# Banded attention with a gated layer: heads regrouped, w_in loaded over 128 partitions, batch 0 turned over in 64x64 blocks

## The chip, the cores and the metric

The kernel runs on one core of a Trainium2 chip. The metric is the device time in microseconds (us) from start to end of one execution. TensorE is the matrix engine, VectorE, ScalarE and GpSimd work on vectors, and SyncE (SP) issues all of the kernel's transfers; 16 DMA engines carry them.

## The reference

Eight batches, 8 heads, 576 positions, head dimension 64. Each query attends to at most 32 keys: its own position and those before it (heads 0 to 3: the last 32 positions; heads 4 to 7: every fourth position of the last 128). The heads' outputs side by side are the input x (576 x 512) of a gated layer.

```python
scores = np.where(masks, scale * q @ k.T, -1e9)
attn = softmax(scores)                      # per head, banded
x = (attn @ v), heads side by side          # B, 576, 512
h = np.maximum(x @ w_in, 0.0)               # 512 -> 1024
u, v = h[..., :512], h[..., 512:]
v_n = (v - mean(v)) / np.sqrt(var(v) + 1e-6)
v_s = w_spatial @ v_n + b_spatial           # mixes the 576 positions
out = (u * v_s) @ w_out                     # 512 -> 512
```

w_in and w_out reach the kernel as 8-byte numbers, so w_in is 4 MB and a half row of 512 numbers is 4096 bytes.

## The kernel before

**Order of the work.** Each piece of work is a Python generator, a strand: `heads_in` and `values_in` (loads), `unit` (scores and softmax), `weighted` (probabilities times values), `v_tile`, `gate` and `project` (the gated layer), `piece_in`, `weight`, `spatial_in`, `spatial`, `weight_in` (loading and splitting of the weights). Class `Timeline` keeps a clock for each engine, with an assumed cost for each step (the numbers behind `yield PE`, `yield ACT` and so on), gives out buffers (eight PSUM banks, four key buffers, six `mid` tiles) and emits the instructions in the order in which its clocks run them. Each strand has a rank; the table SHIFTS moves single ranks, LOADS orders the first loads, BY_POOL and EXTRA choose the engine for some steps (in BY_POOL 'a' and 's' put the addition and the subtraction of the splitting on GpSimd, and without the letter they run on VectorE). The engines work their instructions in that order. All transfers go through SP's one queue, in order as well; an issue waits for its buffer and holds up those behind it.

**Attention.** Heads lie in pairs; `heads_in` loads the keys and queries of a pair, transposed, two heads of 64 rows over 128 partitions, in two transfers (lines 560 and 561). Two pairs form a group; a batch has groups 0 and 1. `unit` computes the scores of a third of a group: 96 products of 64x32 (line 599), maximum, exponential, sum (L689), reciprocal, division (L693). The probabilities have the queries on partitions, 64 of each pair of the group, and along the row first the head j in the pair, then 64 keys. `turn` turns them over with three 128x128 transposes (L614) into one PSUM bank, and ScalarE copies it out (L706). `weighted` (L749) multiplies with the values: the product for head j of the two pairs i = 0, 1 goes to partitions 64 i, so chunk 2G + j of x holds one head of each of two pairs. The values of batch 0 are loaded by pair in four transfers of 32 partitions, both heads' columns to the partitions of each head j, so each byte comes twice (L575). Later batches load only the columns of the head that is used (L586).

**Weights.** As the chunks of x hold the heads in that order, the rows of w_in that belong to a chunk are two blocks of 64 rows that do not adjoin. `piece_in` loads each of the four chunks of each half in two transfers of 64 partitions, the very first block in five parts. `weight` then splits a piece into a high and a low part: two steps on ScalarE (L448, L478), two on VectorE (L452, L454), an addition (L461 on GpSimd or L464 on VectorE), a rounding (L483), a subtraction (L381 or L378). `spatial` splits w_spatial (L510, then L381 or L378). The staging buffers of w_spatial and w_out come free as pieces of w_in are read.

**Gated layer.** Each product is formed in three passes of high and low parts: `v_tile` (L814), `gate` (L881, L891 to L893), `project` (L916). `warm` (L938) fills TensorE at the start with dummy products.

Of the kernel before, what the change touches and what calls it, by code (L numbers as in the profile page):

```python
# [59 lines left out]
LOADS = [0, 1, 3, 20, 2, 10, 21, 4, 5, 15, 8, 6, 13, 9, 12, 18, 7, 22, 23, 11, 19, 17, 26, 24, 16, 14, 25]  # L60
BY_POOL = {
    (0, 0): 's', (0, 1): 'as', (0, 2): 's', (0, 3): 's', (1, 0): 'as', (1, 1): 's',
    (1, 2): 'as', (1, 3): 'a', (2, 0): 'a', (2, 1): 'a', (2, 2): 'as', (2, 3): 'as',
}
EXTRA = {
    ('soft', 0, 0, 0): 0, ('soft', 0, 0, 1): 0, ('soft', 0, 0, 2): 0, ('soft', 0, 1, 0): 0, ('soft', 0, 1, 1): 0, ('soft', 0, 1, 2): 0,
    ('soft', 1, 0, 0): 0, ('soft', 1, 0, 1): 0, ('soft', 1, 0, 2): 0, ('soft', 1, 1, 0): 0, ('soft', 1, 1, 1): 1, ('soft', 1, 1, 2): 1,
    ('sp', 0): 1, ('sp', 1): 1, ('sp', 2): 1, ('sp', 3): 1, ('sp', 4): 1, ('vn', 0): 0,
    ('vn', 1): 1, ('vn', 2): 0, ('vn', 3): 0, ('vn', 4): 1,
# [159 lines left out]
def tile_banded_attention_gated_moe(  # L229
# [157 lines left out]
    def piece_in(half, c):  # L387

        yield DMA, 1.5, 1.1 if half == 0 or c else 2.1
        dtype = w_in.dtype  # L390
        words = NF if dtype == F32 else 2 * NF
        tile = stage[c // 2 + 2 * (1 - half)]
        place = tile[:, c % 2 * BIG :][:, :words] if half else tile[:, c % 2 * words :][:, :words]
        for n in range(2):
            row = (c // 2 * 4 + c % 2 + 2 * n) * D
            cuts = (0, 8, 16, 24, 32, D) if half and c == 0 and n == 0 else (0, D)
            for lo, hi in zip(cuts, cuts[1:]):
                nc.sync.dma_start(  # L398
                    place[n * D + lo : n * D + hi].bitcast(dtype), w_in[row + lo : row + hi, half]
                )  # L400
        staged["wi", half, c] = place
        if half:
            slots["wi", half, c] = [("stage", tile[:, c % 2 * BIG : c % 2 * BIG + BIG])]
        tl.done("in", "wi", half, c)
# [142 lines left out]
    def heads_in(b, hp, lo=0, hi=NU):  # L547

        if lo == 0:
            yield "kq"  # L550
        else:
            yield [("qk", b, hp, lo - 1)]
        got = yield DMA, 0.52 * (hi - lo), 0.87
        if lo == 0:
            used[b, hp] = got
            keys[b, hp] = got[0][1]
        kq = keys[b, hp]
        w = S // NU
        kc = slice(lo * w + WIN * (lo > 0), hi * w + WIN)
        nc.sync.dma_start(kq[:, kc], kT[b, hp, :, kc])  # L560
        nc.sync.dma_start(
            kq[:, WIN + S + lo * w : WIN + S + hi * w].rearrange("p (u c) -> p u c", c=w), qT[b, hp, :, lo:hi]
        )
        for u in range(lo, hi):
            tl.done("qk", b, hp, u)

    def values_in(b, hp):

        if b == 0:
            yield DMA, 1.6, 1.6  # L570
            dst = wide[hp // 2][:, hp % 2 * BIG : hp % 2 * BIG + BIG]
            for j in range(2):
                for n in range(2):
                    k = WIN + (1 - n) * QB
                    nc.sync.dma_start(dst[j * D + n * QB : j * D + n * QB + QB], vw[b, hp, k : k + QB])  # L575
            values[b, hp] = [dst.rearrange("p (t j d) -> p t j d", j=2, d=D)[:, :, j] for j in range(2)]
            tl.done("values", b, hp)
            return
        yield "val"
        (big,) = yield DMA, 1.33, 3.0  # L580
        src = vw[b, hp].rearrange("k (t j d) -> k t j d", j=2, d=D)
        dst = big[1].rearrange("p (t d) -> p t d", d=D)
        for j in range(2):
            for n in range(2):
                k = WIN + (1 - n) * QB
                nc.sync.dma_start(dst[j * D + n * QB : j * D + n * QB + QB], src[k : k + QB, :, j, :])  # L586
        values[b, hp] = [dst, dst]
# [23 lines left out]
    def turn(pp, p, u):  # L611

        for e in range(US):
            nc.tensor.transpose(pp[:, e * P : e * P + P], p[:, e].rearrange("p j k -> p (j k)"), ident)  # L614

    def unit(b, G, u):
# [76 lines left out]
        nc.gpsimd.tensor_mul(flat, flat, rv.unsqueeze(2).broadcast_to([P, 2 * US, KW]))  # L693
        if u:
            yield [("turned", b, G)]
            yield "pt bank"
        else:
            yield "pt bank pT"
        held = yield PE, 0.53, 6
# [3 lines left out]
        turn(held[1][1], p, 0)  # L703
        tl.give(pb)
        yield ACT, 0.48
        nc.scalar.copy(probs[b, G][1][:, u * US * P : u * US * P + US * P], held[1][1][:, : US * P])  # L706
# [5 lines left out]
    def weighted(b, G, rank):  # L712
# [6 lines left out]
        for phase in range(2):  # L719
# [14 lines left out]
            for work_now in itertools.zip_longest(*runs):  # L734
                for odd, h, kb, blocks in filter(None, work_now):
                    row = (1 - odd) * QB
                    for j in (1, 0) if phase else (0, 1):
                        r = slice(j * D + row, j * D + row + QB)
                        for i, hp in enumerate(pairs):
# [5 lines left out]
                            else:  # L745
# [5 lines left out]
                                values[b, hp][j][r, kb // 2],  # L751
# [197 lines left out]
    first += [heads_in(0, 2), heads_in(0, 3), piece_in(1, 0), values_in(0, 0), values_in(0, 1), piece_in(1, 1)]  # L949
    first += [piece_in(1, 2), values_in(0, 2), values_in(0, 3), piece_in(1, 3)] + [piece_in(0, c) for c in range(NC)]  # L950
# [97 lines left out]
```

## Time and profile before

| | us |
|---|---|
| three runs: median (lowest to highest) | 567.3 (565.21 to 569.45) |
| the profiled execution | 566.32 |
| its span, first to last instruction | 564.5 |
| TensorE busy | 540.7 (96%) |
| VectorE busy | 291.1 (52%) |
| ScalarE busy | 222.5 (39%) |
| GpSimd busy | 134.4 (24%) |
| mean granted clock of TensorE, as a share | 0.984 |

Busy times are shares of one span and overlap between engines. Matmuls are pipelined, so a busy TensorE need not be at its peak; a granted clock of 1.00 is 2.4 GHz, 0.50 is 1.2 GHz. What counts is which engine or transfer the others wait for in a stretch, and the stretches differ, so the rows below go by stretch.

### The profile page before, as it was taken

To read this page: it belongs to the slowest core of one execution; us is meant where nothing else is said; L and a number is where in the kernel's file an instruction comes from. 1 tells how busy PE (TensorE), PEld (TensorE's weight loads), DVE (VectorE), ACT (ScalarE), POOL (GpSimd) and SP (SyncE) were. 2 spreads that over 40 slices of the span, in tenths; PEclk is the share of its full clock that TensorE was granted. 3 is DMA by queue.
4 is the path that set the end of the run, shared out by engine and by line. 5 is a ranking of instruction groups with operands and counts; after the bars stand their busy time and mean duration, and the time that the engine had idled before them with its cause. 6 is when DMAs were issued, how large, how long until landed. Compare 5 with 4: busy or idle time off the path is not lost.

```text
span 564.5 us, 18030 instructions
## 1 busy us (share of the span) xinstructions
PE 540.7 (96%) x7838; PEld 496.7 (88%) x7838; DVE 291.1 (52%) x732; ACT 222.5 (39%) x558; POOL 134.4 (24%) x164
## 2 busy tenths in 40 slices
PE   7668988999999999999999999999999999999997
PEld 5446878987999898998998999899999988999997
DVE  6547996547554576555235756566321437314220
ACT  3545765434333353234423344335221424224122
POOL 3446763312223223222001513232100003000000
PEclk9868999999999999999999999999999999999999
DMA  8898622333203424033211342310201100000102
GB/s 244 210 252 226 207 82 88 123 106 79 83 1 121 141 52 134 12 110 129 76 34 27 104 141 66 120 44 2 76 33 43 44 34 1 12 21 12 43 22 74
DMA packets 58818, 48.38 MB, mean 86 GB/s; under 512 B 39154, under 2 KB 48370, under 8 KB 58740
## 3 DMA queue, kind: packets, MB, share of 16 engines
q1 hardware_dynamic: 58740, 47.24, 29.0%
q8 instruction: 61, 1.00, 0.7%
q14 instruction: 17, 0.14, 0.1%
HBM read 37.79 MB, written 9.44 MB: 84 GB/s over the span
## 4 chain that ended last, share of the span: by engine, by line
PE 81%; DMA 10%; DVE 4%; SPq 3%; issue 1%; POOL 1%; ACT 0%; ACTq 0%
PE bank L916 18%; PE bank L891 17%; PE bank L881 17%; PE bank L814 15%; PE bank L749 5%; PE bank L599 4%; DMA kq<-in_qT_dram 3%; DMA wideh<-in_vw_dram 3%; PE bank L614 2%; PE bank L893 1%; PE bank L892 1%; DMA stage<-in_w_spT_dram 1%; DMA wosl<-in_w_in_dram 1%; DMA stage<-in_w_in_dram 1%; SPq L398 1%
## 5 line engine op out<-in xcount | busy, mean ns | idle before, releaser
L881 PE MATMUL bank<-xth,wih 128*128 128x288 f32 x256 | 77.3, 302 | 0.0
L916 PE MATMUL bank<-gh,woh 128*128 128x288 f32 x256 | 77.1, 301 | 0.0
L891 PE MATMUL bank<-wth,vnh 128*128 128x288 f32 x256 | 77.0, 301 | 0.1
L896 DVE TENSOR_TENSOR ur<-ur,bank 128x288 f32<-128x288 f32 x64 | 28.8, 451 | 93.2 <-PE bank L893 90.2
L891 PE MATMUL bank<-wth,vnl 128*128 128x288 f32 x256 | 75.4, 295 | 0.0
L916 PE MATMUL bank<-gl,woh 128*128 128x288 f32 x256 | 75.4, 295 | 0.0
L891 PE MATMUL bank<-wtl,vnh 128*128 128x288 f32 x256 | 75.4, 295 | 0.0
L881 PE MATMUL bank<-xtl,wih 128*128 128x288 f32 x256 | 75.4, 295 | 0.0
L916 PE MATMUL bank<-gh,wol 128*128 128x288 f32 x256 | 75.4, 295 | 0.0
L881 PE MATMUL bank<-xth,wil 128*128 128x288 f32 x256 | 75.4, 294 | 0.0
L832 POOL TENSOR_TENSOR stats<-stats,halfneg 128x1 f32<-128x1 f32 (+1 forms) x37 | 26.2, 709 | 156.8 <-DVE stats L830 156.3
L814 PE MATMUL bank<-wih,xth 128*128 128x512 f32 (+1 forms) x148 | 61.2, 414 | 0.0
L693 POOL TENSOR_TENSOR pg<-pg,rv 128x384 f32<-128x384 f32 x48 | 41.5, 865 | 77.2 <-DVE rv L691 62.7
L814 PE MATMUL bank<-wih,xtl 128*128 128x512 f32 (+1 forms) x148 | 58.6, 396 | 0.0
L814 PE MATMUL bank<-wil,xth 128*128 128x512 f32 (+1 forms) x148 | 58.5, 396 | 0.0
L684 POOL TENSOR_TENSOR pg<-pg,nm 128x384 f32<-128x384 f32 x36 | 30.9, 858 | 113.0 <-DVE nm L682 107.9
L884 ACT ACTIVATE ur<-bank 128x288 f32<-128x288 f32 x64 | 26.3, 412 | 65.3 <-PE bank L881 65.2
L902 ACT CAST gh<-ur 128x288 fp32r<-128x288 f32 x64 | 26.8, 433 | 62.2 <-DVE ur L896 53.2
L891 PEld LDWEIGHTS bank<-wth,vnh 128*128 128x128 f32 x256 | 48.1, 188 | 1.0 <-ACT ur L884 0.3
L916 PEld LDWEIGHTS bank<-gh,woh 128*128 128x128 f32 x256 | 48.1, 188 | 0.9
L881 PEld LDWEIGHTS bank<-xth,wih 128*128 128x128 f32 x256 | 48.1, 188 | 0.7
L920 ACT COPY ob<-bank 128x288 f32<-128x288 f32 x64 | 25.6, 401 | 57.8 <-PE bank L916 48.2
(116 smaller groups left out, 1116.4 us busy)
## 6 DMA issues: line engine op xcount, KB each, us to landing
kq<-in_kT_dram SPq DMA_DIRECT2D x30, 304.0 KB
kq<-in_qT_dram SPq DMA_DIRECT2D x30, 288.0 KB
val<-in_vw_dram SPq DMA_DIRECT2D x112, 72.0 KB
out_dram<-ob SPq DMA_DIRECT2D x48, 144.0 KB
stage<-in_w_out_dram SPq DMA_DIRECT2D x4, 512.0 KB
stage<-in_w_in_dram SPq DMA_DIRECT2D x7, 256.0 KB
out_dram<-ob SPq DMA_DIRECT2D x16, 112.0 KB
stage<-in_w_spT_dram SPq DMA_DIRECT2D x5, 288.0 KB
```

The costliest lines, as they stand in the source:

```text
L684: nc.gpsimd.tensor_add(flat, flat, nm.unsqueeze(2).broadcast_to([P, 2 * US, KW]))
L693: nc.gpsimd.tensor_mul(flat, flat, rv.unsqueeze(2).broadcast_to([P, 2 * US, KW]))
L749: nc.tensor.matmul(acc[h, j][1][1][i * D : i * D + D, at : at + len(blocks) * QB], values[b, hp][j][r, kb // 2], x, start=phase == 0 and k ...
L814: nc.tensor.matmul(pm, xt[a][:, c, at : at + m], wi[w][:, c, NF:], start=c == 0 and n == 0, stop=c == NC - 1 and n == 2)
L832: nc.gpsimd.tensor_tensor(rs[:m], rs[:m], halfneg[:m], op=ALU.pow)
L881: nc.tensor.matmul(pu, wi[w][:, c, fs], xt[a][:, c, xs], start=n == 0, stop=n == 3 * NC - 1)
L884: nc.scalar.activation(ur, pu, AF.Relu)
L891: nc.tensor.matmul(pv, vn[c][a][:, fs], wts[w][:, c, ws], start=n == 0, stop=False)
L896: nc.vector.tensor_mul(ur, ur, pv)
L902: nc.scalar.copy(gated[0][:, f, ts], ur)
L916: nc.tensor.matmul(po, wo[w][:, f, ds], gated[a][:, f, ts], start=n == 0, stop=n == 3 * NC - 1)
L920: nc.scalar.copy(ob[1], po)
```

## The change

Chunk c of x now holds heads 2c and 2c + 1, so a piece of w_in is 128 rows that adjoin, loaded in one transfer over 128 partitions. For this the kernel puts one head of each of two pairs together.
In batches 1 to 7 `heads_in` does it while loading: keys and queries come in four transfers of 64 partitions instead of two of 128, and the values' row blocks now go by pair. In batch 0 (`WHOLE = 1`) keys and queries are loaded as before, and `turn` does the regrouping: 12 products of 64x64 with the identity per unit, into two PSUM banks, each bank's half copied out by itself (two copies of 64 partitions). The values of batch 0 are loaded once per group (8 transfers instead of 16).
The tables are new: SHIFTS, LOADS, BY_POOL (additions on GpSimd: 6 instead of 8; subtractions: 9 as before) and EXTRA (unit ('soft', 1, 1, 1) goes by matrix product, ('sp', 2) to VectorE, ('vn', 0) and ('vn', 1) exchanged, one of the six new copies to VectorE).

```diff
-LOADS = [0, 1, 3, 20, 2, 10, 21, 4, 5, 15, 8, 6, 13, 9, 12, 18, 7, 22, 23, 11, 19, 17, 26, 24, 16, 14, 25]
+LOADS = [0, 1, 3, 2, 19, 5, 6, 4, 17, 18, 7, 9, 10, 20, 12, 16, 14, 15, 23, 8, 22, 11, 21, 13, 24]
 BY_POOL = {
-    (0, 0): 's', (0, 1): 'as', (0, 2): 's', (0, 3): 's', (1, 0): 'as', (1, 1): 's',
-    (1, 2): 'as', (1, 3): 'a', (2, 0): 'a', (2, 1): 'a', (2, 2): 'as', (2, 3): 'as',
+    (0, 0): 'as', (0, 1): 'as', (0, 2): 'as', (0, 3): '', (1, 0): 's', (1, 1): 's',
+    (1, 2): 'as', (1, 3): 's', (2, 0): '', (2, 1): 'as', (2, 2): 'a', (2, 3): 's',
 }
+WHOLE = 1
 ...
     def piece_in(half, c):
 ...
-        for n in range(2):
-            row = (c // 2 * 4 + c % 2 + 2 * n) * D
-            cuts = (0, 8, 16, 24, 32, D) if half and c == 0 and n == 0 else (0, D)
-            for lo, hi in zip(cuts, cuts[1:]):
-                nc.sync.dma_start(
-                    place[n * D + lo : n * D + hi].bitcast(dtype), w_in[row + lo : row + hi, half]
-                )
+        nc.sync.dma_start(place.bitcast(dtype), w_in[c * P : c * P + P, half])
 ...
     def heads_in(b, hp, lo=0, hi=NU):
 ...
+        whole = b < WHOLE
 ...
-        nc.sync.dma_start(kq[:, kc], kT[b, hp, :, kc])
-        nc.sync.dma_start(
-            kq[:, WIN + S + lo * w : WIN + S + hi * w].rearrange("p (u c) -> p u c", c=w), qT[b, hp, :, lo:hi]
-        )
+        rows = slice(hp % 2 * D, hp % 2 * D + D)
+        for to, of, at in ((slice(P), hp, slice(P)),) if whole else (
+            (slice(r * D, r * D + D), hp // 2 * 2 + r, rows) for r in range(2)
+        ):
+            nc.sync.dma_start(kq[to, kc], kT[b, of, at, kc])
+            nc.sync.dma_start(
+                kq[to, WIN + S + lo * w : WIN + S + hi * w].rearrange("p (u c) -> p u c", c=w), qT[b, of, at, lo:hi]
+            )
 ...
     def values_in(b, hp):
+        G, c = divmod(hp, 2)
         if b == 0:
 ...
-            for j in range(2):
-                for n in range(2):
+            dst = wide[G][:, :BIG]
+            for n in range(2):
+                for r in range(2):
                     k = WIN + (1 - n) * QB
-                    nc.sync.dma_start(dst[j * D + n * QB : j * D + n * QB + QB], vw[b, hp, k : k + QB])
+                    nc.sync.dma_start(dst[r * D + n * QB : r * D + n * QB + QB], vw[b, 2 * G + r, k : k + QB])
 ...
-    def turn(pp, p, u):
-        for e in range(US):
-            nc.tensor.transpose(pp[:, e * P : e * P + P], p[:, e].rearrange("p j k -> p (j k)"), ident)
+    def turn(pp, p):
+        if len(pp) == 1:
+            for e in range(US):
+                nc.tensor.transpose(pp[0][:, e * P : e * P + P], p[:, e].rearrange("p j k -> p (j k)"), ident)
+            return
+        for e, j, n in itertools.product(range(US), range(2), range(2)):
+            r = slice(n * D, n * D + D)
+            nc.tensor.matmul(
+                pp[n][r, e * P + j * D : e * P + j * D + D], p[r, e, j], ident[r, r], start=True, stop=True
+            )
 ...
+            nc.scalar.copy(dst[:D], pp[0][:D, : US * P])
+            if EXTRA.get(("turn", *n)):
+                yield DVE, 0.5
+                nc.vector.tensor_copy(dst[D:], pp[1][D:, : US * P])
+            else:
+                yield ACT, 0.48
+                nc.scalar.copy(dst[D:], pp[1][D:, : US * P])
```

## Rows read from the trace of the kernel before

**Rows 1.** Three stretches: busy us of each engine, granted clock, DMA share, GB/s.
```profile
0.00:57.00 57.00, 41.81 (x805) 31.88 (x806) 34.82 (x90) 27.22 (x60) 26.40 (x36) 0.85 0.90 234
57.00:90.00 33.00, 28.90 (x366) 25.40 (x365) 32.15 (x60) 21.99 (x48) 21.71 (x23) 1.00 0.44 143
90.00:564.00 474.00, 470.03 (x6670) 439.40 (x6668) 224.16 (x584) 173.28 (x452) 86.25 (x106) 1.00 0.22 64
```

**Rows 2.** Groups by line: busy us, mean ns | idle before, releaser.
```profile
L938 PE MATMUL bank<-vnl 128*128 128x512 f32 x18 | 7.3, 537 | 1.0 <-DVE vnl L316 1.0
```

**Rows 3.** Waits of TensorE, first 100 us: total us, times, longest.
```profile
PE bank L749 <- DMA wideh<-in_vw_dram: 4.5, 2, 3.7
PE bank L599 <- issue: 2.3, 1, 2.3
```

**Rows 4.** Waits of VectorE and ScalarE, first 57 us.
```profile
DVE mid L452 <- ACT mid L448: 10.2, 4, 5.7
DVE nm L659 <- PE bank L599: 3.0, 2, 1.9
...
ACT mid L448 <- DMA stage<-in_w_in_dram: 8.6, 2, 6.3
```

**Rows 5.** Three more stretches, columns as in rows 1.
```profile
8.00:12.00 4.00, 2.78 (x104) 1.81 (x102) 2.72 (x6) 2.28 (x5) 1.30 (x1) 1.00 1.02 386
24.00:40.00 16.00, 9.82 (x245) 7.41 (x244) 9.13 (x21) 7.59 (x20) 7.62 (x7) 0.68 1.02 235
...
66.50:71.00 4.50, 4.50 (x36) 4.50 (x35) 4.43 (x8) 1.73 (x4) 3.84 (x5) 1.00 0.99 352
```

**Rows 6.** The page's DMA issues, whole span.
```profile
kq<-in_kT_dram SPq DMA_DIRECT2D x30, 304.0 KB
kq<-in_qT_dram SPq DMA_DIRECT2D x30, 288.0 KB
...
stage<-in_w_in_dram SPq DMA_DIRECT2D x7, 256.0 KB
...
wideh<-in_vw_dram SPq DMA_DIRECT2D x8, 144.0 KB
```

**Rows 7.** SP's queue in order of time: start us, length us, issues.
```profile
12.50 9.19 SPq L398 DMA_DIRECT2D stage<-in_w_in_dram  x10
```

**Rows 8.** TensorE in order of time, 20 to 48 us: start, length us, wait before.
```profile
21.59 0.49 PE L614 MATMUL bank<-ident,pg 128*128 128x128 f32 x3
...
31.10 0.48 PE L749 MATMUL bank<-pT,wideh 32*64 32x64 f32 x4 [3.69 <-DMA wideh<-in_vw_dram]
...
36.67 0.90 PE L614 MATMUL bank<-ident,pg 128*128 128x128 f32 x3
...
44.56 0.50 PE L814 MATMUL bank<-wih,xth 128*128 128x512 f32 x1
```

**Rows 9.** GpSimd in order of time: the last division of batch 0.
```profile
30.33 1.12 POOL L693 TENSOR_TENSOR pg<-pg,rv 128x384 f32<-128x384 f32 x1 [0.40 <-DVE rv L691]
```

**Rows 10.** TensorE in order of time, 20 to 48 us, two more.
```profile
22.83 0.76 PE L599 MATMUL bank<-kq 64*32 64x64 f32 x48
...
26.50 0.92 PE L664 MATMUL bank<-nm,ident 128*128 128x192 f32 x4
```

**Rows 11.** Groups by line, whole span, columns as in rows 2.
```profile
L689 DVE TENSOR_REDUCE sm<-pg 128x6 f32<-128x384 f32 x46 | 25.2, 548 | 14.3 <-ACT pg L686 12.8 <-ACT pg L674 1.2
...
L706 ACT COPY pT<-bank 128x384 f32<-128x384 f32 x48 | 22.7, 482 | 25.1 <-PE bank L614 25.0
...
L464 DVE CUSTOM_DVE_ANT_0 mid<-wosl,mid 128x1024 uint16<-128x1024 uint16 x2 | 3.0, 1504 | 2.8 <-ACT wosl L478 2.7
...
L464 DVE CUSTOM_DVE_ANT_0 mid<-stage,mid 128x1024 uint16<-128x1024 uint16 x1 | 0.7, 692 | 0.1
...
L378 DVE TENSOR_TENSOR wil<-mid,wih 128x512 fp32r<-128x512 f32 x1 | 0.7, 665 | 0.0
```

**Rows 12.** Waits of TensorE from 100 us on.
```profile
PE bank L599 <- DMA kq<-in_qT_dram: 0.4, 1, 0.4
```

More of the change, by code (lines that the diff above doesn't have):

```diff
@@ L27 @@
 SHIFTS = {
[29 rows of a table removed]
[29 rows of a table added]
 }
-LOADS = [0, 1, 3, 20, 2, 10, 21, 4, 5, 15, 8, 6, 13, 9, 12, 18, 7, 22, 23, 11, 19, 17, 26, 24, 16, 14, 25]
+LOADS = [0, 1, 3, 2, 19, 5, 6, 4, 17, 18, 7, 9, 10, 20, 12, 16, 14, 15, 23, 8, 22, 11, 21, 13, 24]
 BY_POOL = {
-    (0, 0): 's', (0, 1): 'as', (0, 2): 's', (0, 3): 's', (1, 0): 'as', (1, 1): 's',
-    (1, 2): 'as', (1, 3): 'a', (2, 0): 'a', (2, 1): 'a', (2, 2): 'as', (2, 3): 'as',
+    (0, 0): 'as', (0, 1): 'as', (0, 2): 'as', (0, 3): '', (1, 0): 's', (1, 1): 's',
+    (1, 2): 'as', (1, 3): 's', (2, 0): '', (2, 1): 'as', (2, 2): 'a', (2, 3): 's',
 }
+WHOLE = 1
 EXTRA = {
     ('soft', 0, 0, 0): 0, ('soft', 0, 0, 1): 0, ('soft', 0, 0, 2): 0, ('soft', 0, 1, 0): 0, ('soft', 0, 1, 1): 0, ('soft', 0, 1, 2): 0,
-    ('soft', 1, 0, 0): 0, ('soft', 1, 0, 1): 0, ('soft', 1, 0, 2): 0, ('soft', 1, 1, 0): 0, ('soft', 1, 1, 1): 1, ('soft', 1, 1, 2): 1,
-    ('sp', 0): 1, ('sp', 1): 1, ('sp', 2): 1, ('sp', 3): 1, ('sp', 4): 1, ('vn', 0): 0,
-    ('vn', 1): 1, ('vn', 2): 0, ('vn', 3): 0, ('vn', 4): 1,
+    ('soft', 1, 0, 0): 0, ('soft', 1, 0, 1): 0, ('soft', 1, 0, 2): 0, ('soft', 1, 1, 0): 0, ('soft', 1, 1, 1): 0, ('soft', 1, 1, 2): 1,
+    ('sp', 0): 1, ('sp', 1): 1, ('sp', 2): 0, ('sp', 3): 1, ('sp', 4): 1, ('turn', 0, 0, 0): 0,
+    ('turn', 0, 0, 1): 0, ('turn', 0, 0, 2): 0, ('turn', 0, 1, 0): 0, ('turn', 0, 1, 1): 1, ('turn', 0, 1, 2): 0, ('vn', 0): 1,
+    ('vn', 1): 0, ('vn', 2): 0, ('vn', 3): 0, ('vn', 4): 1,
 }
@@ L387, in piece_in @@
     def piece_in(half, c):
-        yield DMA, 1.5, 1.1 if half == 0 or c else 2.1
+        yield DMA, 1.4, 0.5
         dtype = w_in.dtype
@@ L552, in heads_in @@
             yield [("qk", b, hp, lo - 1)]
-        got = yield DMA, 0.52 * (hi - lo), 0.87
+        whole = b < WHOLE
+        got = yield (DMA, 0.52 * (hi - lo), 0.87) if whole else (DMA, 0.95 * (hi - lo), 1.6)
         if lo == 0:
@@ L567, in values_in @@
     def values_in(b, hp):
+        G, c = divmod(hp, 2)
         if b == 0:
-            yield DMA, 1.6, 1.6
-            dst = wide[hp // 2][:, hp % 2 * BIG : hp % 2 * BIG + BIG]
-            for j in range(2):
-                for n in range(2):
+            yield DMA, 2.4, 1.45
+            dst = wide[G][:, :BIG]
+            for n in range(2):
+                for r in range(2):
                     k = WIN + (1 - n) * QB
-                    nc.sync.dma_start(dst[j * D + n * QB : j * D + n * QB + QB], vw[b, hp, k : k + QB])
-            values[b, hp] = [dst.rearrange("p (t j d) -> p t j d", j=2, d=D)[:, :, j] for j in range(2)]
-            tl.done("values", b, hp)
+                    nc.sync.dma_start(dst[r * D + n * QB : r * D + n * QB + QB], vw[b, 2 * G + r, k : k + QB])
+            for n in range(2):
+                values[b, 2 * G + n] = dst.rearrange("p (t j d) -> p t j d", j=2, d=D)[:, :, n]
+                tl.done("values", b, 2 * G + n)
             return
         yield "val"
-        (big,) = yield DMA, 1.33, 3.0
-        src = vw[b, hp].rearrange("k (t j d) -> k t j d", j=2, d=D)
+        (big,) = yield DMA, 1.33, 3.2
         dst = big[1].rearrange("p (t d) -> p t d", d=D)
-        for j in range(2):
+        for r in range(2):
+            src = vw[b, 2 * G + r].rearrange("k (t j d) -> k t j d", j=2, d=D)
             for n in range(2):
                 k = WIN + (1 - n) * QB
-                nc.sync.dma_start(dst[j * D + n * QB : j * D + n * QB + QB], src[k : k + QB, :, j, :])
-        values[b, hp] = [dst, dst]
+                nc.sync.dma_start(dst[r * D + n * QB : r * D + n * QB + QB], src[k : k + QB, :, c, :])
+        values[b, hp] = dst
         slots["val", b, hp] = [big]
@@ L693, in unit @@
         nc.gpsimd.tensor_mul(flat, flat, rv.unsqueeze(2).broadcast_to([P, 2 * US, KW]))
+        whole = b < WHOLE
         if u:
             yield [("turned", b, G)]
[L696 to L699, printed above, removed]
+        yield "pt bank" + " bank" * whole + " pT" * (u == 0)
+        held = yield (PE, 0.8, 24) if whole else (PE, 0.53, 6)
         if u == 0:
@@ L702, in unit @@
             tl.done("turned", b, G)
-        turn(held[1][1], p, 0)
+        pp = [x[1] for x in held[1:]]
+        turn(pp, p)
         tl.give(pb)
+        dst = probs[b, G][1][:, u * US * P : u * US * P + US * P]
         yield ACT, 0.48
-        nc.scalar.copy(probs[b, G][1][:, u * US * P : u * US * P + US * P], held[1][1][:, : US * P])
+        if not whole:
+            nc.scalar.copy(dst, pp[0][:, : US * P])
+        else:
[3 more added lines that the diff above has]
+                nc.vector.tensor_copy(dst[D:], pp[1][D:, : US * P])
+            else:
+                yield ACT, 0.48
+                nc.scalar.copy(dst[D:], pp[1][D:, : US * P])
         tl.give(*held)
@@ L750, in weighted @@
                                 acc[h, j][1][1][i * D : i * D + D, at : at + len(blocks) * QB],
-                                values[b, hp][j][r, kb // 2],
+                                values[b, hp][r, kb // 2],
                                 x,
@@ L948, in tile_banded_attention_gated_moe @@
     first = [heads_in(0, hp, lo, hi) for lo, hi in ((0, 1), (1, NU)) for hp in (0, 1)]
-    first += [heads_in(0, 2), heads_in(0, 3), piece_in(1, 0), values_in(0, 0), values_in(0, 1), piece_in(1, 1)]
-    first += [piece_in(1, 2), values_in(0, 2), values_in(0, 3), piece_in(1, 3)] + [piece_in(0, c) for c in range(NC)]
+    first += [heads_in(0, 2), heads_in(0, 3), piece_in(1, 0), values_in(0, 0), piece_in(1, 1)]
+    first += [piece_in(1, 2), values_in(0, 2), piece_in(1, 3)] + [piece_in(0, c) for c in range(NC)]
     first += [spatial_in(c) for c in range(5)] + [weight_in(c) for c in range(NC)]
```

58 rows, old and new, of the table SHIFTS are left out of this document.

## The prediction, on record before the changed kernel ran

> **What bounds the kernel now.** I read the table by stretches first [rows 1]. From 90 us to the end TensorE is busy for 470.0 of 474 us: nothing that this change touches can give much there. From 57 to 90 us it is busy for 28.9 of 33 us and VectorE for 32.15 of 33: two engines are full together. In the first 57 us TensorE is busy for 41.8 us only. 7.3 us of that are the 18 dummy products that fill time [rows 2], and the granted clock averages 0.85, so part of the stretch runs at the lower level (1.2 GHz), which costs about 0.15 x 41.8 = 6.3 us. Useful work at the full clock is 41.8 - 7.3 - 6.3 = 28.2 us; the first 57 us waste about 29. That is the pool from which faster loading can draw.
>
> What is waited for there is data. The DMA engines are 0.90 busy through the first 57 us, at 234 GB/s [rows 1]. TensorE's longest wait is for the values (4.5 us), the next is 2.3 us for nothing that is shown [rows 3]. VectorE waits 10.2 us for ScalarE's first step on the pieces of w_in, and ScalarE waits 8.6 us for those pieces to land [rows 4].
>
> **Loads of batch 0.** Equally busy, the DMA engines move 386 GB/s while keys and queries land over 128 partitions (8 to 12 us), but 235 GB/s from 24 to 40 us, when w_in comes in transfers of 64 partitions and values in transfers of 32. The nearest row for the new form of w_in is w_out, 128 rows of 4096 bytes: 352 GB/s from 66.5 to 71 us [rows 5]. By the issues [rows 6] batch 0 fetches 2368 KB of keys and queries (four pairs of 592), 2304 KB of values (16 transfers of 144) and 4096 KB of w_in (16 halves of 256), 8.97 MB, which at 234 GB/s with 2 us to start lasts until about 40 us. After the change 2.42 MB at 386 take 6.3 us, 4.19 MB of w_in at 352 take 11.9 us, and 1.18 MB of values (half as many, still 32 partitions) at 235 take 5.0 us: with the start 25 us, some 15 us sooner. The ten w_in issues that hold SP for 9.2 us [rows 7] become four of about 0.6 us. The values now stand behind the keys and two pieces of w_in: 2 + 6.3 + 3.0 + 5.0 = 16.3 us; I allow 18.
>
> **What that is worth.** Group 0's probabilities were turned over by 22.1 us, but its product with the values began at 31.1 us [rows 8]: 9 us go there. What is late next is the softmax of group 1. Its last probabilities are divided from 30.33 to 31.45 us [rows 9]; even with no speed-up of the softmax they could be turned at once instead of at 36.67, where they stood behind group 0's late product. Group 1's product then needs 2.3 us and its two passes out of PSUM 3, so the steady run of first-layer products, which starts at 44.56 [rows 8], would start near 36.5: 8 us sooner. The softmax should speed up as well. VectorE's two waits for score products, 3.0 us [rows 4], lie in it, and the longer of them ends with the 2.3 us for which TensorE waited for nothing shown; with the DMA engines free earlier I take these 3.0 us as gone (bounds 0 and 4.7, the latter with one wait for w_in). The front moves by 11.0 us. Bounds: 5 us (TensorE's wait for values and little else) and 15 us (all that the data gain).
>
> **The turning in blocks.** In each of six units 12 products of 64x64 replace 3 transposes, and two copies of 64 partitions replace one of 128. No row shows such a product. Below, 48 of 64x32 take 0.76 us [rows 10], so 12 cost 0.2 us; above, 12 without any overlap, each at a third of the 0.49 us that three transposes take [rows 8], cost 2.0 us. A unit's turning now takes 0.5 to 0.9 us, so the difference lies between -0.7 and +1.5 us. I take +0.3, near the 48, because the blocks of the two halves differ in rows and columns as those do. Five of the second copies go to ScalarE and one to VectorE, at most 0.48 us each [rows 11]. ScalarE is busy for 27.2 of the 57 us, which covers them; without that cover the last unit's delay counts, 0.3 + 0.5 = 0.8 us, and I count it. A unit's turning also takes a second of the eight PSUM banks, while group 0's product holds four; that is in the 0.8.
>
> **The replanning.** Two additions in the splitting of w_in and w_out move from GpSimd to VectorE, at 0.7 to 1.5 us [rows 11]: 2.5 us. One subtraction for w_spatial does too (0.75 us, an estimate: 576 columns where 512 take 0.67 us [rows 11]), one softmax unit of batch 1 takes the route by a matrix product (one more reduction on VectorE, 0.55 us; four more products on TensorE, 0.9 us [rows 10, 11]), and the copy adds 0.5. That is 4.4 us of VectorE work. By halves, two additions leave the half of w_in that is used last, two come to the half used first and two to w_out. The front, where VectorE is idle for 22 us, takes up the early ones; in the full stretch I count 2.0 us (bounds 0 and 4.4). TensorE's 0.9 us count as 0.8, as it has gaps there.
>
> **Later batches.** 28 pairs of keys and queries come as four transfers of 64 partitions instead of two of 128, with the same bytes. At 235 instead of 386 GB/s a pair of 592 KB takes 2.6 instead of 1.6 us, and two more issues hold SP for some 0.4 us each: up to 1.8 us later. On SP the outputs and values queue behind them; TensorE awaits the pairs hardly at all, 0.4 us after the first 100 us [rows 12]. Between 0 and 3.6 us (two pairs wholly late); I take 0.3.
> The Trainium skill, SBUF — State Buffer, section "Door 1: The DMA port swizzle", says that partitions 0 to 63 reach no more ports than 0 to 31 and gives 196 GB/s for the 64 against 328 for 128. By that, an estimate, a pair takes 3.1 instead of 1.8 us, and with two pairs late the time would be 563 instead of 559 us. The w_in and w_out rows agree in kind (235 against 352); no run so far shows keys in that form.
>
> **The sum**, against the profiled execution's 566.3 us (span 564.5, and 1.8 around it): 566.3 - 11.0 (front) + 0.8 (turning) + 2.0 (VectorE) + 0.8 (TensorE) + 0.3 (keys) = 559.2, so **559 us**. The median shown, 567.3 of 565.2 to 569.5, is 1.0 us above the profiled execution; I leave that as noise. Under 1% (5.7 us) a change of this kernel can't be told from none.
>
> **Rivals.**
> 1. VectorE takes it back. Its 67.0 us of work up to 90 us become 71.4. If its idle time only shrinks from 23 to 15 us, its full stretch ends at 86 instead of 90 us, and of these 4 us 1 goes to TensorE and keys: 563.5 us. For: it is full from 57 to 90 us [rows 1]. Against: much of its idle time is a wait for what now lands sooner. 16%.
> 2. The wide transfer doesn't do what it says: w_in stays at 235 GB/s, because each row still skips the other half's 4 KB. It then takes 17.8 us, VectorE gets its pieces 6 us later than forecast, and about half of that reaches the end: 562.5 us. 9%.
> 3. Slower: keys and queries of later batches arrive late. If each pair came just in time, 28 x 1.8 = 50 us would be lost; the gain is gone from 4 wholly late pairs on, and with 8 it is over 1% slower, 573 us. For: a lower rate and twice the issues. Against: the DMA engines are 0.22 busy after 90 us [rows 1], and the waits there are 0.4 us [rows 12]. 9%, of which 6% past the 1%.
> 4. More: the data's whole shift passes through and VectorE's idle time in the front falls to 10 us: 566.3 - 15 + 3 = 554 us. 13%.
>
> The forecast, 556 to 562 us, keeps 53%. Faster by over 1% (under 561.6): 0.50 + 0.13 + 0.01 = 0.64; slower by over 1%: 0.06; within: 0.30. The range goes down to 552, rival 4 with the early additions hidden, and up to 565, over rivals 1 and 2; outside are the losses in later batches and part of the near-zero gains.
>
> **What would show it.** Right: over 330 GB/s while w_in lands, its last piece in before 29 us, no wait of TensorE for values, first-layer products steady from 33 to 38 us, and from 90 us on the same stages about 7 us earlier with TensorE's busy time within 1 us. The turning: 12 products in at most 1.2 us. Wrong: w_in at 235 GB/s; VectorE idle for over 15 us before its full stretch ends; TensorE waiting over 3 us for keys after the first 100 us. Group 1's product starting after 35 us would refute the part on the softmax.

## The result and the profile after

| | before | after |
|---|---|---|
| median of four runs, us | 566.42 | 559.46 |
| lowest to highest, us | 565.21 to 569.45 | 559.04 to 560.86 |
| profiled execution, us (its span) | 566.32 (564.5) | 559.76 (558.0) |

The ratio is 0.9874, with a 95% interval of 0.9828 to 0.9919: faster by 1.3%, 7 us, at the place the forecast named (559).

The stretches of the changed kernel (busy us of each engine with its instructions, granted clock, DMA share, GB/s; the first three answer to [rows 1], the last three are new):

```profile
0.00:57.00 57.00, 46.38 (x999) 35.68 (x1000) 38.47 (x102) 31.99 (x71) 25.79 (x36) 0.91 0.79 219
57.00:90.00 33.00, 28.33 (x332) 26.38 (x330) 29.65 (x59) 22.97 (x56) 18.53 (x21) 1.00 0.48 146
90.00:558.00 468.00, 463.38 (x6629) 433.45 (x6627) 223.38 (x578) 168.26 (x427) 84.56 (x105) 1.00 0.23 64
12.00:22.00 10.00, 6.91 (x181) 5.34 (x181) 4.38 (x12) 5.37 (x13) 1.94 (x2) 0.97 1.03 225
22.00:28.00 6.00, 4.28 (x64) 3.48 (x60) 4.57 (x10) 3.27 (x9) 3.33 (x3) 0.57 1.01 400
28.00:32.00 4.00, 2.69 (x113) 2.25 (x119) 2.99 (x6) 1.71 (x6) 2.24 (x2) 0.79 1.01 216
```

Read the last three by their rates; the DMA engines are equally full in all of them. From 22 to 28 us, when w_in alone lands over 128 partitions, they move 400 GB/s. From 12 to 22 us, with w_in beside the values (still 32 partitions a transfer), they move 225; from 28 to 32 us, when batch 1's keys and queries come in their new form of 64 partitions, 216. w_in is in by about 28 us, where the rate drops, instead of about 40.

TensorE in order of time (start, length us, what, wait before):

```profile
21.32 0.91 PE L622 MATMUL bank<-ident,pg 64*64 64x64 f32 x22 [1.62 <-ACT pT L720]
24.46 0.94 PE L602 MATMUL bank<-kq 64*32 64x64 f32 x46 [1.72 <-issue]
28.19 1.50 PE L769 MATMUL bank<-pT,wideh 32*64 32x64 f32 x72
31.00 0.91 PE L622 MATMUL bank<-ident,pg 64*64 64x64 f32 x24 [1.31 <-POOL wil L383]
...
35.70 0.50 PE L834 MATMUL bank<-wih,xth 128*128 128x512 f32 x1
...
38.67 1.05 PE L769 MATMUL bank<-pT,widel 32*64 32x64 f32 x72
...
41.60 0.50 PE L834 MATMUL bank<-wih,xth 128*128 128x512 f32 x1
...
54.51 0.39 PE L834 MATMUL bank<-wih,xtl 128*128 128x512 f32 x1
...
68.03 0.40 PE L911 MATMUL bank<-wth,vnh 128*128 128x288 f32 x1
...
100.12 0.40 PE L936 MATMUL bank<-gh,woh 128*128 128x288 f32 x1
...
554.56 0.29 PE L936 MATMUL bank<-gh,wol 128*128 128x288 f32 x1
```

Lines have moved: L769 is the product with the values, L622 the turning in blocks, L834 the first layer (before: L749, L614, L814 [rows 8]). A product of 64x64 stands as two records, so a unit's 12 products are 24; the unit at 21.32 had its first product at 19.37. Group 0's product starts at 28.19 instead of 31.10 us with no wait for values. The first layer starts at 35.70 instead of 37.23; group 1's product cuts into it at 38.67, as before at 38.62, and it runs steadily from 41.60 instead of 44.56. Batch 0's last first-layer product starts at 54.51, the first spatial product at 68.03, the first projection at 100.12, the last product at 554.56; before these were 62.47, 73.39, 106.23 and 560.90. So 8.0 us are gained by the end of the first layer, and about 6 from there to the end.

The waits of TensorE in the first 100 us, and from 100 us on (total us, times, longest), answering to [rows 3, 12]:

```profile
PE bank L674 <- DVE nm L669: 3.5, 2, 2.2
PE bank L602 <- issue: 2.3, 2, 1.7
PE bank L622 <- ACT pT L720: 1.6, 1, 1.6
...
PE bank L769 <- issue: 1.0, 1, 1.0
PE bank L618 <- POOL pg L703: 0.2, 1, 0.2
PE bank L769 <- DMA val<-in_vw_dram: 0.2, 1, 0.2
```

VectorE's and ScalarE's waits in the first 57 us, answering to [rows 4]:

```profile
DVE mid L448 <- ACT mid L444: 4.7, 3, 2.6
DVE nm L669 <- PE bank L602: 3.0, 3, 1.2
...
ACT mid L444 <- DMA stage<-in_w_in_dram: 7.8, 2, 4.0
```

VectorE's wait for split pieces of w_in fell from 10.2 to 4.7 us. Its wait for scores did not fall: 3.0 us, as before.

### The profile page after: what moved, and what is told of

It is laid out like the page before. It is cut to its first block, busy times and chain, and to the rows that moved or that the text cites. A ratio compares the mean times of both kernels' runs of the same rounds, so it can differ in the third digit from the quotient of the medians.

```text
span 558.0 us, 18320 instructions
## 1 busy us (share of the span) xinstructions
PE 538.1 (96%) x7956; PEld 495.5 (89%) x7956; DVE 291.5 (52%) x737; ACT 223.2 (40%) x552; POOL 128.9 (23%) x161
## 4 chain that ended last, share of the span: by engine, by line
PE 86%; DVE 5%; DMA 4%; ACT 2%; issue 2%; SPq 1%; POOL 1%; DVEq 0%; ACTq 0%; POOLq 0%
PE bank L936 18%; PE bank L901 17%; PE bank L911 17%; PE bank L834 17%; PE bank L769 6%; PE bank L602 4%; PE bank L618 3%; DMA stage<-in_w_in_dram 2%; PE bank L913 1%; PE bank L912 1%; DVE mid L450 1%; DMA kq<-in_qT_dram 1%; DMA stage<-in_w_spT_dram 1%; DMA val<-in_vw_dram 1%; PE bank L622 0%
## 5 line engine op out<-in xcount | busy, mean ns | idle before, releaser
L852 POOL TENSOR_TENSOR stats<-stats,halfneg 128x1 f32<-128x1 f32 (+1 forms) x37 | 24.0, 652 | 188.2 <-DVE stats L850 187.9
L834 PE MATMUL bank<-wih,xth 128*128 128x512 f32 (+1 forms) x148 | 59.9, 405 | 0.0
L834 PE MATMUL bank<-wih,xtl 128*128 128x512 f32 (+1 forms) x148 | 57.9, 391 | 0.0
L834 PE MATMUL bank<-wil,xth 128*128 128x512 f32 (+1 forms) x148 | 57.9, 391 | 0.0
```

Of the source, the lines that this page charges most:

```text
L834: nc.tensor.matmul(pm, xt[a][:, c, at : at + m], wi[w][:, c, NF:], start=c == 0 and n == 0, stop=c == NC - 1 and n == 2)
L852: nc.gpsimd.tensor_tensor(rs[:m], rs[:m], halfneg[:m], op=ALU.pow)
```

## The experiments

Each kernel ran beside the kernel before. They came in three sets of four, each set on one chip; between sets ratios are compared.

**1. w_in in halves of 64 partitions again.**

```diff
-        nc.sync.dma_start(place.bitcast(dtype), w_in[c * P : c * P + P, half])
+        for n in range(2):
+            row = c * P + n * D
+            nc.sync.dma_start(place[n * D : n * D + D].bitcast(dtype), w_in[row : row + D, half])
```

> The changed kernel with each piece of w_in loaded in two transfers of 64 partitions again, its planned order untouched. Theory (the gain is earlier data): w_in falls from 405 to about 240 GB/s where it is alone (22 to 28 us of the changed kernel), the last piece lands 3 to 4 us later and the time rises by 2 to 4 us, to 561.5 to 563.5 us. Rival (the new tables make the gain, the loads don't matter): within 1 us of 559.5. Rival (VectorE sets the end of the front): the time rises by 1 us or less although the data are 3 us later.

564.64 us, ratio 0.9955 (0.9934 to 0.9977). From 20 to 30 us, mostly w_in:

```profile
20.00:30.00 10.00, 7.66 (x306) 6.33 (x288) 7.75 (x15) 6.91 (x17) 6.40 (x6) 0.92 0.97 248
```

The same bytes from the same rows to the same places move at 248 instead of 400 GB/s, and half or more of the gain is gone: 0.0047 to 0.0081 of the time, 2.7 to 4.6 us, against the two ratios of the changed kernel (0.9908 in run 5 below, and 0.9874). The halves are also smaller transfers, of 256 KB; but the keys and queries before, of 304 and 288 KB over 128 partitions, moved at 386 GB/s [rows 5, 6], so their size is not what slows them.

**2. The values of batch 0 fetched twice**, the second time into columns that nothing reads.

```diff
+            for n in range(2):
+                for r in range(2):
+                    k = WIN + (1 - n) * QB
+                    nc.sync.dma_start(wide[G][r * D + n * QB : r * D + n * QB + QB, BIG : 2 * BIG], vw[b, 2 * G + r, k : k + QB])
             for n in range(2):
                 values[b, 2 * G + n] = dst.rearrange("p (t j d) -> p t j d", j=2, d=D)[:, :, n]
```

> The changed kernel with the values of batch 0 loaded a second time, into columns that nothing reads: 1.18 MB more in transfers of 32 partitions, in the same place of SP's queue. Theory: at 220 to 235 GB/s everything behind them is 5 us later and the time rises by 3 to 5 us, to 562.5 to 564.5 us. Rival (tables): within 1 us of 559.5. Rival (VectorE): up by 1 us or less.

564.43 us, ratio 0.995 (0.9926 to 0.9973): the 1.18 MB cost as much as the halves. The intervals of runs 1 and 2 overlap that of run 5 (0.9875 to 0.9941), so neither loss stands alone against it; the next run's does.

**3. Both at once**, under the changed kernel's tables.

> Both: w_in in transfers of 64 partitions and the values twice, in the changed kernel's order. Theory: the gain of 7 us is gone, 565 to 569 us. Rival (tables): 560 to 561 us. If the two effects overlap rather than add, 563 to 565 us.

567.39 us, ratio 0.9994 (0.9974 to 1.0013). Two stretches, and TensorE's longest wait:

```profile
20.00:30.00 10.00, 9.36 (x239) 7.61 (x236) 7.54 (x18) 5.44 (x13) 4.63 (x4) 0.73 0.92 247
30.00:40.00 10.00, 4.64 (x146) 4.26 (x143) 4.66 (x10) 4.93 (x13) 2.88 (x3) 0.61 1.03 255
```

```profile
PE bank L775 <- ACT turnstile L788: 4.1, 1, 4.1
```

That wait is for a small copy on ScalarE: ScalarE stands still for 5.5 us before its step on a piece of w_in (until 33.96 us), and the copy comes behind that step (34.52). Data lands at some 250 GB/s until 40 us, as it did before, and the whole gain is gone, with the new tables, the turning and the new order of heads all in place. A better plan as the source of the gain, a rival here, falls; that the plan pays for what the turning in blocks costs (run 7) is not excluded, for this run has both.

**4. The kernel before, with w_in's rows put in order in memory**, so that each piece is one transfer of 128 partitions; nothing else is changed.

```diff
-        for n in range(2):
-            row = (c // 2 * 4 + c % 2 + 2 * n) * D
 ...
+        nc.sync.dma_start(place.bitcast(dtype), w_in[c * P : c * P + P, half])
 ...
-        "w_in": raw(moe_w_in),
+        "w_in": raw(np.concatenate([moe_w_in[g * 64 : g * 64 + 64] for g in (0, 2, 1, 3, 4, 6, 5, 7)], 0)),
```

> The kernel before with one part alone: the rows of w_in are laid out in memory in the order of the chunks, so that each piece is one transfer of 128 partitions; heads, turning, values and planned order stay. Theory: the w_in part of the load falls from about 17.5 to 11 us, of which 2 to 4 us reach the end: 562.5 to 564.5 us against 566.4. Rival (tables): no change within 1 us. Rival (the values alone were late, and w_in waits on nothing): at most 1 us, since the values of group 0 land only 1.4 us earlier.

563.6 us, ratio 0.9923 (0.9889 to 0.9957). TensorE still waits 1.8 us for values, which come twice here:

```profile
PE bank L743 <- DMA wideh<-in_vw_dram: 1.8, 2, 1.0
```

So the wide w_in alone, with the kernel before's turning and tables, gives more than half of what the change gives (0.8 of 1.3%; its interval is 0.4 to 1.1%).

**5. The changed kernel once more**, for the next three to be compared with.

> The changed kernel itself, as the reference for the runs beside it on one chip: 559 to 561 us, 6 to 8 us below the kernel before.

562.47 us (558.56 to 564.42), above the 559 to 561 that were expected, ratio 0.9908 (0.9875 to 0.9941): the ratio of the first result lies in this interval and this one in that, but the single runs of one kernel differ by 5.9 us. The profiled execution is the longest one, 564.42 us:

```profile
30.00:40.00 10.00, 7.86 (x150) 6.83 (x147) 5.65 (x13) 6.81 (x15) 2.10 (x2) 0.50 0.57 133
```

```profile
29.22 1.54 PE L622 MATMUL bank<-ident,pg 64*64 64x64 f32 x24 [3.02 <-issue]
```

TensorE waits 3.0 us for nothing that the profile shows before a turning, and then has the lower clock (0.50, 1.2 GHz) from 30 to 40 us; in the first result's profile that stretch ran at 1.00.

**6. Keys and queries of batches 1 to 7 put in order in memory**, so that they come in two transfers of 128 partitions as before; the same function regroups `kT`.

```diff
-        for to, of, at in ((slice(P), hp, slice(P)),) if whole else (
-            (slice(r * D, r * D + D), hp // 2 * 2 + r, rows) for r in range(2)
-        ):
+        for to, of, at in ((slice(P), hp, slice(P)),):
 ...
+    def regrouped(x):
+        G = x.shape[1] // 2
+        y = x.reshape(B, G, 2, 2, D, *x.shape[3:]).swapaxes(2, 3).reshape(x.shape)
+        return np.concatenate([x[:1], y[1:]], 0)
+
+    qT = regrouped(qT)
```

> The changed kernel with keys and queries of batches 1 to 7 laid out in memory by regrouped heads, so that each pair comes in two transfers of 128 partitions instead of four of 64; planned order untouched. Theory (they are hidden): faster by 0 to 1 us. Rival (half the rate and twice the issues delay TensorE): faster by 2 us or more, at least the 1.2 us of TensorE's waits for keys in the first 100 us of the changed kernel.

560.95 us, ratio 0.9902 (0.9874 to 0.9931), the same as run 5. The narrow keys are slow (216 GB/s above) and cost nothing that can be measured.

**7. Batch 0 regrouped in memory too**, so that a unit is turned by three transposes and one copy.

```diff
-        if len(pp) == 1:
+        if True:
 ...
-            nc.scalar.copy(dst[:D], pp[0][:D, : US * P])
+            nc.scalar.copy(dst, pp[0][:, : US * P])
 ...
-        return np.concatenate([x[:1], y[1:]], 0)
+        return np.concatenate([x[:0], y[0:]], 0)
```

> As the run before, and batch 0 regrouped in memory as well: its probabilities are turned over by three 128x128 transposes into one bank and copied out once (both banks stay reserved, the order stays). Theory: the turning in blocks costs 0.8 us, so this is 0.5 to 1.5 us faster than the run with wide keys. Rival (the block turning is what holds up the softmax of batch 0, by the second copy on ScalarE): 2 to 4 us faster.

558.4 us, ratio 0.9847 (0.9827 to 0.9867). Against run 6, whose interval begins at 0.9874, the blocks cost 2.5 us by the medians, 1.9 by the lowest runs and 3.1 by the ratios: the rival's size (2 to 4 us) and not the theory's, but that the second copy on ScalarE makes it is not shown. TensorE, at the full clock:

```profile
12.43 0.49 PE L616 MATMUL bank<-ident,pg 128*128 128x128 f32 x3
...
37.25 1.05 PE L767 MATMUL bank<-pT,widel 32*64 32x64 f32 x72
```

**8. Values in one transfer of 128 partitions** in the changed kernel, in every batch (the edit for batch 0 is shown), their rows in order in memory.

```diff
-            for n in range(2):
-                for r in range(2):
-                    k = WIN + (1 - n) * QB
-                    nc.sync.dma_start(dst[r * D + n * QB : r * D + n * QB + QB], vw[b, 2 * G + r, k : k + QB])
+            nc.sync.dma_start(dst, vw[b, 2 * G : 2 * G + 2].rearrange("r k c -> (r k) c"))
 ...
+    vw = np.concatenate([vw[:, :, 64:], vw[:, :, 32:64]], 2)
```

> The changed kernel with the values laid out in memory so that a group's (in later batches a pair's) come in one transfer of 128 partitions instead of four of 32; bytes and planned order untouched. Theory: from 12 to 22 us, where values and w_in share the DMA engines at 220 GB/s, the rate rises to 370 or more, the data are 4 us earlier and the time falls by 1.5 to 4 us, to 555.5 to 558 us. Rival (VectorE, or the softmax of batch 0, now sets the front): within 1 us.

559.45 us (556.6 to 562.51; a sixth execution, 566.19, is not in the ratio), ratio 0.9867 (0.9834 to 0.99), not told apart from run 5. The rate while values and w_in land, ScalarE's wait for w_in, and group 1's product:

```profile
10.00:20.00 10.00, 9.30 (x244) 7.33 (x236) 7.14 (x21) 6.50 (x16) 3.16 (x4) 1.00 1.02 404
```

```profile
ACT mid L444 <- DMA stage<-in_w_in_dram: 3.7, 2, 3.1
```

```profile
37.01 1.05 PE L763 MATMUL bank<-pT,widel 32*64 32x64 f32 x72
```

The mechanism is plain (404 instead of some 225 GB/s, and against the first result's profile the wait 3.7 instead of 7.8 us, group 1 1.7 us sooner); its worth in the whole time is not shown, for the runs spread over 6 us.

**9. Everything put in order in memory**: runs 6, 7 and 8 together, the version that they point to.

> The changed kernel's order with everything regrouped in memory: keys, queries and values of every batch in transfers of 128 partitions, batch 0 turned over by three 128x128 transposes and one copy per unit. Theory (all loads of the front wide, and no block turning): at least as fast as the better of its two parts, 554 to 558 us. Rival (the front is bound by VectorE and code loading by now): 557 to 560 us, no gain over either part.

557.03 us (555.54 to 558.01), ratio 0.9834 (0.9814 to 0.9853), with run 11 the best of all that ran, faster than the kernel before by 1.7%. Against the changed kernel's 0.9908 (0.9875 to 0.9941) the intervals lie apart, against its 0.9874 (0.9828 to 0.9919) they don't; the two never ran in one set. The stretch in which w_in and values land:

```profile
10.00:20.00 10.00, 9.63 (x223) 7.62 (x223) 6.61 (x20) 5.94 (x14) 2.91 (x4) 1.00 1.03 407
```

**10. Two dummy products of 512 columns before each turning of the changed kernel**, overwritten by it; the theory was that TensorE's low clock makes the spread.

```diff
     def turn(pp, p):
+        if len(pp) == 2:
+            for _ in range(2):
+                nc.tensor.matmul(
+                    pp[0].rearrange("p (n c) -> p n c", n=4), zeros, zeros.unsqueeze(1).broadcast_to([P, 4, P]), start=True, stop=True
+                )
```

> The changed kernel with two dummy products of 512 columns ahead of each of the six turnings of batch 0, where TensorE waits for probabilities (12 products, about 0.43 us each at full clock; their results are overwritten). Theory (the spread of 558.6 to 564.4 us between executions is where the stretch at the lower clock falls, and it falls after TensorE has waited): less time at 0.50 between 20 and 42 us, and a median of 558 to 560 us with a narrower spread. Rival (the clock follows the wait for code, which no product can fill): spread and median unchanged, or up to 2 us slower from the added products.

563.61 us (559.39 to 566.62), ratio 0.9945 (0.9921 to 0.9969): no faster, no narrower. The profiled execution:

```profile
20.00:30.00 10.00, 7.86 (x198) 6.19 (x182) 6.08 (x14) 5.11 (x13) 4.65 (x5) 0.68 1.03 338
30.00:40.00 10.00, 8.23 (x167) 6.06 (x165) 6.20 (x12) 5.13 (x13) 2.19 (x2) 0.63 0.62 154
```

The clock still falls to the lower level for part of both stretches. The remedy failed; what puts the clock where it falls stays open. Here it falls at 23.7 us, inside a wait of TensorE of 2.1 us that stands in the middle of a turning (22.0 to 24.2 us), where no product placed ahead could fill it.

**11. The same dummies in the version of run 9.**

> The same dummy products in the kernel with everything regrouped in memory. Theory (clock): 0 to 2 us faster than that kernel, clock 1.00 through the turnings. Rival (they are only more work on the way): 0.5 to 2 us slower.

556.79 us, ratio 0.9835 (0.9815 to 0.9854): no difference.

**12. The version of run 9 with the two additions for w_out on GpSimd** again.

```diff
-            nc.vector.tensor_add(f, g, low)
+            (nc.gpsimd if key[0] == "wo" else nc.vector).tensor_add(f, g, low)
```

> The kernel with everything regrouped in memory, with the two additions for w_out that the new tables put on VectorE done by GpSimd, at the same places of the order. Theory of the prediction (VectorE's added work costs 2.0 us in its full stretch): 1 to 2 us faster than that kernel. Rival (the addition on VectorE takes only 0.7 us when GpSimd is idle, and GpSimd takes twice that): no change within 1 us, or slower.

557.47 us, ratio 0.9842 (0.9824 to 0.9861): no difference. The step in the version of run 9 from 60 to 90 us, by line, and then here:

```profile
L460 DVE CUSTOM_DVE_ANT_0 mid<-stage,mid 128x1024 uint16<-128x1024 uint16 x2 | 1.4, 692 | 0.2
```

```profile
L460 POOL TENSOR_TENSOR mid<-mid,stage 128x512 uint32<-128x512 uint32 x2 | 2.7, 1329 | 0.7 <-issue 0.7
```

## Why the prediction was right, and where its terms were not

**The cause was right.** The gain is loading: w_in over 128 partitions and the values once. Run 3 takes both away and the gain with them; run 4 adds the first alone to the kernel before and gets over half. By their ratios runs 1 and 2 each lose 2.4 to 4.6 us or so of the 5.2 to 7.1 that the change gave. The way from the loads to the end of the first layer was not the one that the forecast took, as follows.

**Data, point by point.** More than 330 GB/s were wanted for w_in, and 400 are there where it is alone; the forecast took 352 from the w_out row. It priced w_in and values one after the other; they landed together at 225. These errors have opposite signs: the last piece was in at about 28 us (forecast 25; the line drawn was 29).
The Trainium skill, SBUF — State Buffer, section "Door 1: The DMA port swizzle", has 64 partitions reach no more ports than 32. The traces agree in kind: 216 GB/s for keys over 64 partitions, 248 for w_in over 64, about 225 with 32-partition values in the mix, and 400 to 407 over 128. The same page of the Trainium skill, SBUF — State Buffer, section "Can I just issue two DMAs to hit both halves?", says that two transfers, one on each half, don't make up for one over 128. Run 1, with two halves one behind the other, agrees: 248.

**The softmax of group 1: refuted.** The term "I take these 3.0 us as gone" failed, and so did the path through group 1's product. That product began at 38.67 us, past the 35 that was set and no sooner than before. The kernel before:

```profile
37.23 0.79 PE L814 MATMUL bank<-wih,xth 128*128 128x512 f32 x1
...
38.62 1.05 PE L749 MATMUL bank<-pT,widel 32*64 32x64 f32 x72
...
41.63 0.35 PE L749 MATMUL bank<-pT,widel 32*64 32x64 f32 x11 [1.06 <-ACT turnstile L762]
43.71 0.92 PE L749 MATMUL bank<-pT,widel 32*64 32x64 f32 x69 [1.73 <-issue]
...
62.47 0.40 PE L814 MATMUL bank<-wih,xtl 128*64 128x512 f32 x1
```

There too the first layer began ahead of group 1's product, with 3 of batch 0's 60 products; now 12 go ahead of it. The steady run starts at 41.60 instead of 44.56 us, outside the 33 to 38 that was set. These 3.0 us are about the two waits (1.06 and 1.73 us) in which group 1's product stood still before, and which the forecast's chain left out. Counted from the rows, the 8.0 us at the end of the first layer are these 3.0, 2.1 for nine more products done before the steady run (0.23 us each), 1.6 because the steady run no longer has a stretch at the lower clock (45.1 to 48.8 us before), and 1.3 for the rest. Group 0's product, where the forecast saw 9 us go, came 2.9 us sooner.

VectorE waited 3.0 us for scores as before, now in three waits (0.77, 1.24 and 0.98 us). The last two end with scores that TensorE began late, after 0.54 us (before 16.35) and 1.72 us (before 24.46) of waiting for nothing shown, 2.3 us together as before:

```profile
25.47 0.62 DVE L669 TENSOR_REDUCE nm<-bank 128x3 f32<-128x192 f32 x2 [0.98 <-PE bank L602]
```

The forecast let these waits go with the load on the DMA engines; they stayed (the last section has what they follow). The other delay is ScalarE's order. It takes its instructions in turn; its step on the second piece of w_in (L444) stood ahead of a unit's copies (L720, L726) and of two exponentials (L684), and it stood still for it (start, length us, wait before):

```profile
12.34 0.67 ACT L444 ACTIVATE mid<-stage 128x512 f32<-128x512 f32 x1 [3.81 <-DMA stage<-in_w_in_dram]
...
20.25 0.66 ACT L444 ACTIVATE mid<-stage 128x512 f32<-128x512 f32 x1 [4.00 <-DMA stage<-in_w_in_dram]
20.80 0.46 ACT L720 COPY pT<-bank 64x384 f32<-64x384 f32 x1
21.29 0.47 ACT L726 COPY pT<-bank 64x384 f32<-64x384 f32 x1
21.79 0.55 ACT L684 ACTIVATE pg<-bank 128x192 f32<-128x192 f32 x2
```

The piece for the step at 20.25 was issued at 9.27 us, landed at 20.22 and shared the DMA engines with values over 32 partitions. TensorE's 1.62 us inside its turning, before 21.32, are a wait for the copy that stood behind that step. In run 8, where the values don't slow w_in, ScalarE's wait is 3.7 instead of 7.8 us and group 1's product starts at 37.01.

**The turning: too cheap.** I took 0.8 us for six units; run 7 against run 6 gives 1.9 to 3.1. A unit's 12 products take 0.91 to 0.94 us at the full clock, and three transposes 0.49 to 0.55. My reason for +0.3 a unit, the 48 products of 64x32 in 0.76 us [rows 10], made one unit's blocks about right (+0.4), but I let only the last unit's delay count. Nor was the second bank free: TensorE's wait of 1.6 us for a copy comes after a unit's first product (19.37 us) and before its second, which goes to the other bank; the copy that empties it stood behind the step on w_in above. What the second copy costs is not shown. Run 7 also has 252 fewer instructions for TensorE, and that may be part of the price (last section). The rows of the turning and of the additions:

```profile
L622 PE MATMUL bank<-ident,pg 64*64 64x64 f32 x144 | 5.8, 223 | 4.0 <-ACT pT L720 1.6 <-POOL wil L383 1.3 <-ACT xth L810 1.1
L460 DVE CUSTOM_DVE_ANT_0 mid<-stage,mid 128x1024 uint16<-128x1024 uint16 x5 | 3.9, 778 | 0.4
```

**VectorE's 2.0 us: not there.** The last row above has the additions at 0.78 us each; [rows 11] had one at 0.69 beside two at 1.50, and I priced them by the dear ones. In the traces of the kernel before, the changed kernel and runs 7, 8, 9 and 12 the dear ones are those with a GpSimd instruction beside them: such an addition took 0.69 us without one (22 times) and 0.78 to 1.55 us with one (10 times). VectorE's busy time over the whole execution went from 291.1 to 291.5 us, not up by 4.4. The sign set for rival 1 did appear: VectorE is idle for 19.1 of the first 60 us. But nothing followed from it, for it is idle for data that are late in that stretch, and it had done 64.1 us of work by 84 us, where its full stretch now ends, against 67.0 by 90 us before. Run 12 moves two of the additions back without effect, though in the version of run 9, not in this one.

**TensorE and keys: as forecast.** From 83.9 us to the end TensorE is idle for 4.6 us, before from 90 us for 4.0: within 1 us. No wait for keys is seen after 100 us, and run 6 finds no gain in widening them. They land at 216 GB/s; the 563 us that I gave for two late pairs did not come, for none was late. The stages from 90 us on are 6.1 to 6.3 us earlier (forecast: about 7).

**The sum.** The front of the first layer moved by 8.0 us with the turning's cost already in it, against 10.2 forecast (11.0 - 0.8). Of 3.1 us that were to be given back later, 1.6 were (8.0 to 6.3). The gain of the front was put too high and the costs behind it too high as well; the turning, put too low, is part of the first error. So the time was hit more closely than its terms, by luck: the errors, 2.2 and 1.5 us, have opposite signs. Two slips change little. TensorE's longest wait in total was not for the values (4.5 us) but for GpSimd's divided probabilities (4.7 us in the first 100, 1.5 of it in the front), and VectorE's added work adds up to 4.3, not 4.4 us.

## What to carry to other kernels

Compare the GB/s of stretches in which the DMA engines are equally full: where they differ by 1.7, give the early loads all 128 partitions, best by the order of rows in memory, since regrouping on TensorE took back some 2 to 3 us here. Where an engine works in order, look for the step that waits for a transfer in front of other work, and at what else shares the DMA engines with that transfer. A term that two rows price differently should be taken with both prices, and the wider one tested first. A wait for nothing shown should not be counted as gained before it is known what ends it.

## What was not expected of the hardware

Runs of one kernel can differ by 1%: the changed kernel ran from 558.56 to 564.42 us in one set and from 559.04 to 560.86 in another. The versions with three transposes of runs 7, 9, 11 and 12 stayed within 1.6 to 2.5 us; the turning alone is not the reason, for the kernel before and run 4, which have transposes too, spread over 5.5 and 6.6 us, and run 1, with blocks, over 1.5. The two profiled executions of the changed kernel differ in when TensorE waits for nothing shown (1.7 us before 24.46 in one, 3.0 before 29.22 in the other) and in where the clock is 0.50: in both the lower level begins inside that wait, at 22.9 and at 28.0 us, but it lasts until 29.7 in one and 41.7 in the other, and there batch 0's last first-layer product starts at 58.09 instead of 54.51 us. Such waits recur in most profiles while the DMA engines are full, 3.6 us in that of run 9:

```profile
PE bank L761 <- issue: 3.6, 1, 3.6
```

They have a sign in common. The page of the changed kernel lists a DMA queue for instructions (packets, MB, share of 16 engines):

```profile
q8 instruction: 62, 1.02, 0.8%
```

These are packets of 16 KB, one for about 257 of TensorE's 15,912 matmuls and weight loads (x7956 each on the page); run 7, with 252 fewer, has 61. In all fourteen profiles together TensorE waits for `issue` 39 times after the first 5 us, for 0.2 to 3.6 us, and each time the wait ends 1.2 to 1.7 us after such a packet has landed: at 23.05 us with TensorE starting at 24.46 in the first result, at 27.88 and 29.22 in run 5, at 27.15 and 28.75 in run 9. So TensorE most likely waits there for its own instructions. Most packets have no such wait behind them, and no run was made to vary this; it stays a coincidence in time, if one without exception. It would give the turning in blocks a second price: before 40 us five packets land in the changed kernel and four in run 7. Why some kernels spread less was not settled.

Narrow transfers beside wide ones bring down the rate of the whole: 225 GB/s with values of 32 partitions in the mix (12 to 22 us), 404 when the values too have 128 (run 8, 10 to 20 us). How much of that the wide transfer itself loses was not measured apart.
